# F on its own hardware queue, k quads in column tiles, and w2 and w3 of the first chunk by contraction halves in a Linformer attention and maxout kernel

## The chip, the cores and the metric

One core of one Trainium2 chip. The metric is the device time of one execution in microseconds (us), the median of several. The span that a profile shows is some 1.8 us shorter than that time.

## The reference, cut to what matters

```python
# batch 8, heads 8, sequence 1024, head_dim 64, k_proj 64
k_proj = np.einsum('ks,bhsd->bhkd', E, k)        # E, F: (64, 1024)
v_proj = np.einsum('ks,bhsd->bhkd', F, v)
attn   = softmax(q @ k_proj.T / 8)
x      = attn @ v_proj                           # -> (8192, 512)
h      = max(max(x @ w1, x @ w2), x @ w3)        # w1..w3: (512, 768)
out    = h @ w_out                               # (768, 512)
```

## The kernel before: the parts that matter

Batches are taken one after the other, each in two chunks of 512 tokens. While batch b runs through the maxout layer, the attention of batch b+1 is slipped in between its steps. Only the start is special: nothing can be overlapped with batch 0, so its first chunk has its own code, and all three edits are in it.

The loads of batch 0, in the order of issue. All but E and F go through POOL's software queue:

```python
    nc.sync.dma_start(out=ef_f[0:KP], in_=E)
    nc.sync.dma_start(out=ef_f[KP:P], in_=F)
    # ... on POOL: q and k (4 heads at a time), v of heads 0-1, 2-3, 4-5
    load_w(0, slice(0, 2))            # w1, first half of the contraction
    load_kv(2, V3)                    # v of heads 6-7
    load_w(0, slice(2, 3)); load_w(0, slice(3, 4))
    load_w(1, slice(0, 2)); load_w(1, slice(2, 4))      # w2
    load_w(2, slice(0, 2))                              # w3, first half
    load_q(ALL, slice(SPC, SI))                         # q of the second chunk
    load_w(2, slice(2, 4))                              # w3, second half
    # ... w_out, then batch 1            (written one call to a line in the kernel)
```

The k projection of four heads, its transpose, and the start of the front. `idle(n)` is n filler matmuls on a tile of zeros, there to keep PE's clock up:

```python
    def k_duo(u):
        t, ns = bank()
        for si in range(SI):
            nc.tensor.matmul(out=t[0:KP, 0:4 * D], lhsT=efT[:, si, 0:KP],
                             rhs=k_t[:, 4 * u:4 * u + 4, si, :], ...)
        kp0[u] = att.tile([KP, 4 * D], BF16, name="kp0")
        copy("v", kp0[u], t[0:KP, 0:4 * D], ns, 0.45)
    # kt_duo: two transposes of kp0, one copy
    k_duo(0); q_duo(1); kt_duo(0); idle(1)
    # scores of two head pairs, their sums; then the second four heads, v, ...
```

The first chunk of the maxout layer (`NJT` = 6 column tiles jt, `NCT` = 4 contraction tiles ct). The first weight goes ct by ct; the other two go jt by jt, and VectorE takes the running maximum from the PSUM bank as each jt ends. Keys such as `(2, 5)` name the step behind which attention work of the second chunk is put:

```python
        for i in (1, 2):                                  # w2, w3
            for jt in jts:
                t, ns = bank()
                up_mm(t, i, 0, 0, jt, range(NCT))
                most(hs[:, jt] if i == 1 else hTs[0, 0][:, jt, :], t, ns, hs[:, jt])
                then((i, jt))
        # work: (2, 0), (2, 1): transposes of q (qp); (2, 2), (2, 3): scores (sc);
        # (2, 5): sums, values, and the multiply into xT on VectorE (za), scores
```

The softmax here doesn't subtract the row's maximum and nothing guards it: scores larger than these inputs give would overflow.

## Time and profile before

| | |
|---|---|
| time, median of 3 | 409.4 us (409.08 to 409.49) |
| span, PE busy | 407.8 us, 394.0 us (97%) |
| granted TensorE clock | 0.997 |

The page of the kernel before. Its last line here is a group of equal instructions: behind the first bar its busy time in us and the mean of one in ns, behind the second how long the engine stood idle just before them, and what ended most of that:

```profile
span 407.8 us, 5967 instructions
PE 394.0 (97%) x2381; PEld 180.1 (44%) x2425; DVE 201.5 (49%) x309; ACT 191.2 (47%) x278; POOL 31.4 (8%) x44
...
L502 PE MATMUL banks<-xT,w_sb 128*128 128x512 bf16 x1118 | 254.6, 379 | 2.6 <-DMA w_sb<-in_moe_w_dram 0.6
```

PE is the bound, so a gain can come only from time in which PE stands or does filler. The chain of waits of the kernel before, first 50 us (start, length, what):

```profile
6.35 0.66 POOL v_t L143
7.01 13.44 DMA w_sb<-in_moe_w_dram
20.45 0.28 issue
20.73 13.09 DMA w_sb<-in_moe_w_dram
33.82 0.04 issue
33.87 0.61 PE banks L502 x2
...
48.39 0.99 PE banks L280 x16
```

From 7.01 to 33.87 us it is the load stream, and from then on mostly PE. The timeline of the kernel before (start, length, engine, line, operation, tiles, shapes, and in brackets the idle time before it):

```profile
10.91 1.03 PE L402 MATMUL banks<-k_t,efT 128*64 128x256 bf16 x8 [0.62 <-DMA k_t<-in_k_dram]
11.98 0.42 DVE L99 CAST kp<-banks 64x256 bf16<-64x256 f32 x1 [1.94 <-PE banks L402]
12.23 0.64 PE L291 MATMUL banks<-ident,q_t 128*64 128x128 bf16 x16 [0.28 <-DMA q_t<-in_q_dram]
12.80 0.23 PE L415 MATMUL banks<-ident,kp 64*128 64x64 bf16 x2
12.91 0.69 DVE L99 COPY qT<-banks 128x1024 bf16<-128x1024 bf16 x1 [0.51 <-PE banks L291]
13.51 0.21 DVE L99 COPY kpT<-banks 128x128 bf16<-128x128 bf16 x1
13.78 0.41 PE L199 MATMUL banks<-qT,kpT 64*64 64x256 bf16 x8 [0.76 <-DVE kpT L99]
...
21.51 2.10 PE L502 MATMUL banks<-xT,w_sb 128*128 128x512 bf16 x9
...
33.87 0.61 PE L502 MATMUL banks<-xT,w_sb 128*128 128x512 bf16 x2 [0.62 <-DMA w_sb<-in_moe_w_dram]
```

The k projection (10.91) waits for k; the transpose of its result (12.80) waits behind transposes of q, which wait for q, and the copy of that (13.51) behind the copy of q's transposes on VectorE (12.91); the first up matmul (21.51) comes 1.06 us after w1's first half landed (20.45); and in the middle of w3 PE stands for its second half.

Throughout this text a load "lands" when the last of the sixteen counts of its semaphore arrives, as the trace records them.

### The profile page before, as it was taken

The numbers are of one execution on the slowest core, as the hardware profiler recorded it, in microseconds if no ns is written. First come the engines' busy times: TensorE is split into PE (matmuls) and PEld (weight loads), VectorE is DVE, ScalarE is ACT, GpSimd is POOL, SyncE is SP. The second block draws the span as 40 slices with busy tenths as digits, with TensorE's granted clock in tenths as the row PEclk, the third lists the DMA queues.
The fourth block names the chain that finished last, engine by engine and source line by source line (L and its number), as shares of the span: only waits on it lengthen the run. The fifth ranks groups of instructions, "written<-read, shape, count | busy, mean of one in ns | idle before, by whom it ended". The sixth has DMA issues, their size and how long they took to land.

```text
span 407.8 us, 5967 instructions
## 1 busy us (share of the span) xinstructions
PE 394.0 (97%) x2381; PEld 180.1 (44%) x2425; DVE 201.5 (49%) x309; ACT 191.2 (47%) x278; POOL 31.4 (8%) x44
## 2 busy tenths in 40 slices
PE   7899999999999999999999999999999999999995
PEld 2543453344444544444544445444544444444443
DVE  2357665473565527636453555525464363525251
ACT  2531538624764266556544555437535555432322
POOL 7421002002000200200200002000000000000000
PEclk9999999999999999999999999999999999999998
DMA  8999939949916994892798119950510202020202
GB/s 150 205 205 207 232 88 154 250 113 139 245 30 190 172 251 110 130 241 45 207 181 179 54 24 244 204 147 2 139 70 1 104 0 104 0 104 0 103 2 104
DMA packets 58508, 52.30 MB, mean 128 GB/s; under 512 B 25968, under 2 KB 54128, under 8 KB 58480
## 3 DMA queue, kind: packets, MB, share of 16 engines
q0 software_dynamic: 28512, 28.31, 43.6%
q1 hardware_dynamic: 29824, 23.46, 17.6%
q8 instruction: 19, 0.31, 0.3%
q10 hardware_dynamic: 144, 0.13, 0.1%
q14 instruction: 9, 0.07, 0.1%
HBM read 57.15 MB, written 16.78 MB: 181 GB/s over the span
## 4 chain that ended last, share of the span: by engine, by line
PE 87%; DMA 7%; ACT 2%; POOL 1%; issue 1%; DVE 1%; DVEq 0%; ACTq 0%; POOLq 0%
PE banks L502 58%; PE banks L593 19%; DMA w_sb<-in_moe_w_dram 7%; PE banks L219 4%; PE banks L280 3%; PE banks L199 2%; PE banks L291 1%; POOL v_t L143 1%; DMA out_dram<-o_sb 0%; ACT zi L238 0%; ACT zl L232 0%; POOL k_t L143 0%; ACT pT L210 0%; POOL q_t L148 0%; DVE hT L512 0%
## 5 line engine op out<-in xcount | busy, mean ns | idle before, releaser
L502 PE MATMUL banks<-xT,w_sb 128*128 128x512 bf16 x1118 | 254.6, 379 | 2.6 <-DMA w_sb<-in_moe_w_dram 0.6
L502 PEld LDWEIGHTS <-w_sb 128*128 128x128 bf16 x1152 | 109.7, 98 | 137.6 <-issue 10.1
L558 DVE TENSOR_TENSOR m<-banks,h1s 128x512 f32<-128x512 f32 x90 | 62.0, 689 | 86.0 <-ACT h1s L554 54.6
L554 ACT COPY h1s<-banks 128x512 f32<-128x512 f32 x90 | 52.5, 583 | 92.5 <-PE banks L502 89.2
L593 PE MATMUL banks<-wout_sb,hT 128*128 128x512 bf16 x370 | 85.0, 379 | 0.9 <-issue 0.3
L249 DVE TENSOR_TENSOR xT<-banks,zi 128x1024 bf16<-128x1024 f32 (+1 forms) x36 | 39.8, 1106 | 77.2 <-ACT zi L238 57.9
L512 DVE TENSOR_TENSOR hT<-banks,m 128x512 bf16<-128x512 f32 x90 | 62.3, 692 | 10.1 <-DVE m L558 0.5
L99 ACT COPY o_sb<-banks 128x512 f32<-128x512 f32 (+1 forms) x60 | 34.9, 581 | 53.3 <-PE banks L593 53.2
L593 PEld LDWEIGHTS <-hT 128*128 128x128 bf16 x378 | 35.9, 98 | 45.9 <-DVE hT L512 3.3
L232 ACT ACTIVATE zl<-banks 128x1024 f32<-128x1024 f32 (+1 forms) x36 | 33.5, 930 | 30.9 <-PE banks L219 30.7
L210 ACT ACTIVATE pT<-banks 128x1024 bf16<-128x1024 f32 (+1 forms) x36 | 33.2, 931 | 15.3 <-PE banks L199 15.3
L238 ACT ACTIVATE zi<-zl 128x1024 f32<-128x1024 f32 (+1 forms) x36 | 34.6, 962 | 1.1
L188 POOL DMA_DIRECT2D q_t<-in_q_dram x7 | 6.1, 878 | 205.1 <-DMA qT<-q_p 108.1
L219 PE MATMUL banks<-pT,ones 64*64 64x512 bf16 (+1 forms) x144 | 13.9, 376 | 0.9 <-DVE xT L249 0.3
L199 PE MATMUL banks<-qT,kpT 64*64 64x512 bf16 (+1 forms) x144 | 13.0, 359 | 1.1 <-DVE kpT L99 0.8
L219 PE MATMUL banks<-pT,vp 64*64 64x512 bf16 (+1 forms) x144 | 13.3, 355 | 0.2
L280 PEld LDWEIGHTS <-efT 128*64 128x64 bf16 x224 | 11.7, 110 | 2.7 <-issue 2.7
L219 PEld LDWEIGHTS <-ones 64*64 64x64 bf16 x144 | 4.4, 103 | 15.1 <-issue 14.7
L99 DVE CAST vp<-banks 64x256 bf16<-64x256 f32 (+1 forms) x18 | 7.1, 395 | 5.8 <-ACT vp L99 3.4
L373 PE MATMUL banks<-warm 128*128 128x512 bf16 x23 | 8.5, 502 | 1.2 <-DVE warm L166 1.2
L99 ACT CAST vp<-banks 64x256 bf16<-64x256 f32 x14 | 5.1, 365 | 7.3 <-PE banks L280 7.1
L99 DVE COPY q_p<-q_t 128x1024 bf16<-128x1024 bf16 x24 | 8.5, 419 | 0.0
(48 smaller groups left out, 107.0 us busy)
## 6 DMA issues: line engine op xcount, KB each, us to landing
out_dram<-o_sb SPq DMA_DIRECT2D x30, 512.0 KB, 3.5
k_t<-in_k_dram POOLq DMA_DIRECT2D x7, 1024.0 KB, 14.4
q_t<-in_q_dram POOLq DMA_DIRECT2D x7, 1024.0 KB, 9.7
v_t<-in_v_dram POOLq DMA_DIRECT2D x7, 1024.0 KB, 18.7
w_sb<-in_moe_w_dram POOLq DMA_DIRECT2D x5, 384.0 KB, 11.7
k_t<-in_k_dram POOLq DMA_DIRECT2D x2, 512.0 KB, 9.9
v_t<-in_v_dram POOLq DMA_DIRECT2D x4, 256.0 KB, 12.3
wout_sb<-in_moe_w_out_dram POOLq DMA_DIRECT2D x1, 768.0 KB, 15.6
```

The costliest lines, as they stand in the source:

```text
L99: done = {"v": nc.vector.tensor_copy, "s": nc.scalar.copy, "g": nc.gpsimd.tensor_copy}[eng](out=o, in_=i)
L210: nc.scalar.activation(out=pTs[b, g, lo], in_=t, func=AF.Exp, scale=scale)
L219: nc.tensor.matmul(out=t[hp * HALF:(hp + 1) * HALF, c, 0:nsi * HALF], lhsT=w(rows, hp), rhs=p[rows, hp, :], start=True, stop=True,)
L232: nc.scalar.activation(out=zl, in_=t, func=AF.Ln)
L238: nc.scalar.activation(out=zi, in_=zl, func=AF.Exp, scale=-1.0)
L249: nc.vector.tensor_tensor(out=xTs[b][:, g, lo:lo + nsi, :].rearrange("a (c s) p -> a c (s p)", c=2), in0=t, in1=zi, op=ALU.mult,)
L280: nc.tensor.matmul(out=t[hh * HALF:(hh + 1) * HALF, 0:width], lhsT=efT[:, si, (kv - 1) * KP:kv * KP], rhs=qkv[b][kv][:, heads[hh], si, :], ...
L502: nc.tensor.matmul(out=h, lhsT=w_sb[i][:, ct, jt * P:(jt + 1) * P], rhs=xTs[b][:, ct, ch * SPC:(ch + 1) * SPC, :], start=(ct == first), st ...
L512: nc.vector.tensor_tensor(out=o, in0=h, in1=other, op=ALU.max)
L554: nc.scalar.copy(out=h1s, in_=h[0][0])
L558: nc.vector.tensor_tensor(out=m12, in0=h[1][0], in1=h1s, op=ALU.max)
L593: nc.tensor.matmul(out=o_ps, lhsT=hTs[b, ch][:, jt, tt * P:(tt + 1) * P], rhs=wout_sb[:, jt, :], start=(jt == 0), stop=(jt == NJT - 1),)
```

## The change

"k quads" is the name for the k projection of four heads in two column tiles: two of the heads are written to rows 0 to 63 of the result and two to rows 64 to 127, where all four went to rows 0 to 63 before. "The halves" are w2 and w3 of the first chunk, done by halves of the contraction.

Intent: have E and F in sooner, shorten the way to the first scores and hence to the first up matmul, and give PE work that does not need w3's second half until it has landed.

```diff
-    nc.sync.dma_start(out=ef_f[KP:P], in_=F)
+    nc.scalar.dma_start(out=ef_f[KP:P], in_=F)
 # k_duo: two column tiles, each two heads of the four
-        for si in range(SI): nc.tensor.matmul(out=t[0:KP, 0:4 * D], ...)
-        kp0[u] = att.tile([KP, 4 * D], BF16, name="kp0")
+        proj(0, 1, t, (slice(4 * u, 4 * u + 2), slice(4 * u + 2, 4 * u + 4)), 2 * D)
+        kp0[u] = att.tile([P, 2 * D], BF16, name="kp0")
 # kt_duo: one 128x128 transpose instead of two
 # the front
     k_duo(0)
-    at(10.3)
-    q_duo(1)
+    idle(2)
     kt_duo(0)
     idle(1)
     # ... scores of two head pairs
-    idle(2)
+    at(10.6)
+    q_duo(1)
 # w2 and w3 of the first chunk
         for i in (1, 2):
+            h = []
             for jt in jts:
-                t, ns = bank()
-                up_mm(t, i, 0, 0, jt, range(NCT))
-                most(..., t, ns, hs[:, jt])
+                h.append(bank())
+                up_mm(h[jt][0], i, 0, 0, jt, range(NCT // 2))
+                then((i, "a", jt))
+            for jt in jts:
+                up_mm(h[jt][0], i, 0, 0, jt, range(NCT // 2, NCT))
+                most(..., *h[jt], hs[:, jt])
                 then((i, jt))
 # attention work behind them: (2, 0), (2, 1) -> (2, "a", 2), (2, "a", 5);
 # (2, 2), (2, 3), (2, 5) -> (2, 0), (2, 2), (2, 4)
```

More of the change, by code (lines that the diff above doesn't have):

```diff
@@ L400, in k_duo @@
         t, ns = bank()
-        for si in range(SI):
-            nc.tensor.matmul(
-                out=t[0:KP, 0:4 * D], lhsT=efT[:, si, 0:KP],
-                rhs=k_t[:, 4 * u:4 * u + 4, si, :],
-                start=(si == 0), stop=(si == SI - 1),
-            )
-        pe(0.9)
-        kp0[u] = att.tile([KP, 4 * D], BF16, name="kp0")
-        copy("v", kp0[u], t[0:KP, 0:4 * D], ns, 0.45)
+        proj(0, 1, t, (slice(4 * u, 4 * u + 2), slice(4 * u + 2, 4 * u + 4)), 2 * D)
+        kp0[u] = att.tile([P, 2 * D], BF16, name="kp0")
+        copy("v", kp0[u], t[:, 0:2 * D], ns, 0.3)
     def kt_duo(u):
@@ L413, in kt_duo @@
         t = t.bitcast(BF16)
-        for gg in range(2):
-            nc.tensor.transpose(
-                out=t[:, gg * KP:(gg + 1) * KP],
-                in_=kp0[u][:, gg * P:(gg + 1) * P], identity=ident[0:KP, 0:KP],
-            )
+        nc.tensor.transpose(out=t[:, 0:P], in_=kp0[u], identity=ident)
         pe(0.15)
@@ L421, in kt_duo @@
             "v", kpTs[0][:, 2 * u:2 * u + 2, :].rearrange("a g k -> a (g k)"),
-            t[:, 0:2 * KP], ns, 0.25,
+            t[:, 0:P], ns, 0.25,
         )
@@ L475 @@
     z(1)
+    idle(1)
     at(12.8)
@@ L479 @@
     kt_duo(1)
-    at(14.3)
+    at(14.1)
     v_pair(0)
@@ L533, in up_first @@
         for i in (1, 2):
+            h = []
             for jt in jts:
-                t, ns = bank()
-                up_mm(t, i, 0, 0, jt, range(NCT))
-                most(hs[:, jt] if i == 1 else hTs[0, 0][:, jt, :], t, ns, hs[:, jt])
+                h.append(bank())
[3 more added lines that the diff above has]
+                up_mm(h[jt][0], i, 0, 0, jt, range(NCT // 2, NCT))
+                most(hs[:, jt] if i == 1 else hTs[0, 0][:, jt, :], *h[jt], hs[:, jt])
                 then((i, jt))
@@ L683 @@
                     (0, 1, 5): [lambda: x(3)],
-                    (2, 0): [qp(0, (0, 1), *c1)],
-                    (2, 1): [qp(0, (2, 3), *c1)],
-                    (2, 2): [sc(0, 0, *c1)],
-                    (2, 3): [sc(0, 1, *c1)],
-                    (2, 5): [za(0, 0, *c1), sc(0, 2, *c1)],
+                    (2, "a", 2): [qp(0, (0, 1), *c1)],
+                    (2, "a", 5): [qp(0, (2, 3), *c1)],
+                    (2, 0): [sc(0, 0, *c1)],
+                    (2, 2): [sc(0, 1, *c1)],
+                    (2, 4): [za(0, 0, *c1), sc(0, 2, *c1)],
                 })
```

## The prediction

> **What bounds the kernel now.** TensorE: the page gives PE 394.0 of 407.8 us busy, clock 0.997. Of the 13.8 us idle, 6.1 lie in the first 60 us (busy time by stretches). All three edits act in the first 42 us. There the load stream bounds: the software queue moves some 205 GB/s without a pause from 7 to 48 us, and the chain of waits is a w_sb load from 7.0 to 20.5 and another from 20.7 to 33.8. In the timeline PE follows landings: k projection at 10.91 (k landed 10.87), first up matmul 21.51 (w1 half landed 20.45), and a stall to 33.87 for the second half of w3 (landed 33.83).
>
> **The change, costed.**
>
> 1. F on its own queue. F was issued at 1.38, its packets flowed from 3.6 to 5.2, after E's, and it landed at 7.07; in 4.0 to 5.2 the software queue got only about 60 KB where it later moves 200 KB/us. The Trainium skill ("DMA: Bandwidth & Descriptors", Queues, rings and completion order) says SP and ACT each own a row of rings on the same 16 engines. So E and F should flow together from 2.2 and F land near 5. The engine work is not less; it fills a half-empty start. Estimate: every later load lands 0.6 us earlier (0.2 to 0.8), w3's second half near 33.2. The E/F transposes then wait for the identity (POOL, 6.35): 6.4 instead of 7.83, but the k projection still waits for k, about 10.3.
>
> 2. k quads. Eight 128x256 matmuls in 1.03 us become 16 of 128 columns, in pairs of column tiles, about 0.55 us (32 of 256 columns take 1.87 elsewhere); the copy 0.42 -> 0.29; one transpose for two. And q_duo(1), which waited for q until 12.23 and held the k transpose back to 12.80, moves behind the scores. First scores 13.78 -> 11.9, second 17.86 -> about 15.9. But first up then waits for w1 (20.45 - 0.6): 21.51 -> 19.9. These two steps together bring PE 1.6 us forward; the loads set it.
>
> 3. ct halves. 12 matmuls (2.6 us) of w3 stand before its second half is needed, so the stall to 33.87 (PE group 0.62 idle, PEld 1.1) goes. No arithmetic changes. But results come in bunches: w2's six maxima (0.69 each, 0.61 to 0.79 apart) fall due within 2.6 us of PE, so VectorE runs about 2 us behind. The second q transpose must wait for a pair of banks (six are open), and the last hT maximum stands behind a 0.69 us xT multiply that waits for ScalarE. PE arrives at the first down step about 2 us early and there waits, I estimate, 0.7 us before its sixth matmul; another 0.3 to 0.4 us is lost at the scores.
>
> **On the path.** About 2 us won by 40 us, half given back to VectorE: 1.0 us kept. After that all is paced by PE and moves along (k, q, v of batch 1 land 4 to 5 us before use).
>
> **Time: 408.4 us**, 407.6 to 409.1 (8 in 10). Faster by over 2%: 0.01; within 2%: 0.98; slower: 0.01.
>
> **Right or wrong.** F landing 4.5 to 5.3; w3's second half at 33.0 to 33.5 and no PE wait for it; first up matmul 19.6 to 20.2; in the first down step a wait for DVE hT, 0.4 to 1 us; the first k projection of batch 1 (48.39) at 47.2 to 47.7; every later stage the same length.
>
> **What would make it wrong.** The load stream not shifting (gain 0.4 or less); VectorE keeping up better, so the whole 2 us stays (407.4); bank waits worse than I count (no gain). If ACT's issue delays its table load or casts, it is hidden.

## The result, and the profile after

| | before | after |
|---|---|---|
| time, median of 4 | 409.28 us | 408.63 us (408.55 to 409.40) |
| ratio, 95% interval | | 0.9988 (0.9971 to 1.0006) |

A ratio here is the mean time of one kernel's fast runs over that of the other's fast runs of the same rounds, so it is not quite the ratio of the medians. The interval includes 1: by these runs alone the kernels are the same. The change was run twice more below; over the three times, 15 executions of it have a mean of 408.90 us and the 24 of the kernel before beside them 409.15 us, each with a scatter (standard deviation) of 0.42 us. So the question is not why the gain is large or small, but what lies under a quarter of a microsecond of net gain: parts that cancel, or parts that do nothing.

The page of the changed kernel, profiled in the slowest of those four executions:

```profile
span 407.6 us, 5997 instructions
PE 393.7 (97%) x2395; PEld 180.1 (44%) x2440; DVE 201.1 (49%) x309; ACT 191.2 (47%) x278; POOL 31.5 (8%) x44
...
L588 PE MATMUL banks<-wout_sb,hT 128*128 128x512 bf16 x370 | 85.1, 379 | 1.6 <-DVE hT L503 0.9
```

The down matmuls now stand 1.6 us in all, 0.9 of it for hT on VectorE; in the kernel before it was 0.9 us, the largest part of which, 0.3, was for nothing the profile shows. (L493 and L588 here are L502 and L593 of before, L503 is L512.) Its timeline:

```profile
10.49 0.64 PE L280 MATMUL banks<-k_t,efT 128*64 128x128 bf16 x16 [1.11 <-DMA k_t<-in_k_dram]
11.16 0.29 DVE L99 CAST kp<-banks 128x128 bf16<-128x128 f32 x1 [2.04 <-PE banks L280]
11.51 0.23 PE L408 MATMUL banks<-ident,kp 128*128 128x128 bf16 x1
11.78 0.23 DVE L99 COPY kpT<-banks 128x128 bf16<-128x128 bf16 x1 [0.33 <-PE banks L408]
12.06 0.41 PE L199 MATMUL banks<-qT,kpT 64*64 64x256 bf16 x8
12.40 0.64 PE L291 MATMUL banks<-ident,q_t 128*64 128x128 bf16 x16
...
20.79 2.12 PE L493 MATMUL banks<-xT,w_sb 128*128 128x512 bf16 x9
...
30.06 3.68 DVE L503 TENSOR_TENSOR hs<-banks,hs 128x512 f32<-128x512 f32 x6 [2.07 <-PE banks L493]
...
36.73 0.30 PE L199 MATMUL banks<-qT,kpT 64*64 64x256 bf16 x4 [0.25 <-DVE qT L99]
...
40.23 1.24 PE L588 MATMUL banks<-wout_sb,hT 128*128 128x512 bf16 x5
40.83 0.69 DVE L249 TENSOR_TENSOR xT<-banks,zi 128x512 bf16<-128x512 f32 x1 [0.73 <-ACT zi L238]
41.44 0.68 DVE L503 TENSOR_TENSOR hT<-banks,hs 128x512 bf16<-128x512 f32 x1
42.18 0.39 PE L588 MATMUL banks<-wout_sb,hT 128*128 128x512 bf16 x1 [0.70 <-DVE hT L503]
```

The first scores come 1.7 us sooner than before (12.06 against 13.78). VectorE stands 2.07 us for lack of a finished bank and then takes six maxima in a row. Five matmuls of the first down step run at 40.23, and the sixth stands 0.70 us for the last hT maximum, which stood behind a multiply that waited for ScalarE.

### The whole run in four pieces

The traces of all runs let the run be cut at three points: the first up matmul of the first chunk, the first k projection of batch 1 (at 48.3 us in the kernel before), and the last matmul. The last long piece, from that k projection to the last matmul, is 354.99 to 355.02 us in **every one** of the fourteen profiles. So all that the change does must be in the first two pieces:

| us | first up matmul at | from there to the k projection of batch 1 | from there to the last matmul | end |
|---|---|---|---|---|
| before | 21.51 | 26.81 | 354.99 | 4.5 |
| after, three profiles | 20.79, 20.32, 20.03 | 27.30, 27.29, 27.29 | 355.0 | 4.5 to 4.6 |

The first piece became shorter by 0.7 to 1.5 us and scatters; the second became **longer** by 0.48 us and scatters by 0.01. The experiments take these apart.

### The profile page after: what moved, and what is told of

It reads as the page before. It is cut to its first block, busy times and chain, and to the rows that moved or that the text cites. A ratio compares the mean times of both kernels' runs of the same rounds, so it can differ in the third digit from the quotient of the medians.

```text
span 407.6 us, 5997 instructions
## 1 busy us (share of the span) xinstructions
PE 393.7 (97%) x2395; PEld 180.1 (44%) x2440; DVE 201.1 (49%) x309; ACT 191.2 (47%) x278; POOL 31.5 (8%) x44
## 4 chain that ended last, share of the span: by engine, by line
PE 89%; DMA 4%; ACT 2%; DVE 2%; issue 2%; POOL 1%; DVEq 0%; ACTq 0%; POOLq 0%
PE banks L493 60%; PE banks L588 19%; PE banks L219 4%; PE banks L280 3%; DMA v_t<-in_v_dram 3%; PE banks L199 2%; DVE hT L503 1%; PE banks L291 1%; ACT zl L232 1%; DMA out_dram<-o_sb 0%; ACT zi L238 0%; POOL k_t L143 0%; ACT pT L210 0%; POOL q_t L148 0%; POOL v_t L143 0%
## 5 line engine op out<-in xcount | busy, mean ns | idle before, releaser
L493 PE MATMUL banks<-xT,w_sb 128*128 128x512 bf16 x1118 | 254.5, 379 | 2.1 <-issue 0.6
L493 PEld LDWEIGHTS <-w_sb 128*128 128x128 bf16 x1152 | 109.5, 98 | 136.8 <-issue 10.1
L588 PE MATMUL banks<-wout_sb,hT 128*128 128x512 bf16 x370 | 85.1, 379 | 1.6 <-DVE hT L503 0.9
L503 DVE TENSOR_TENSOR hT<-banks,m 128x512 bf16<-128x512 f32 x90 | 62.3, 692 | 10.1 <-DVE m L553 0.5
L588 PEld LDWEIGHTS <-hT 128*128 128x128 bf16 x378 | 36.0, 98 | 46.9 <-DVE hT L503 4.4
L210 ACT ACTIVATE pT<-banks 128x1024 bf16<-128x1024 f32 (+1 forms) x36 | 33.2, 931 | 14.7 <-PE banks L199 14.7
L280 PEld LDWEIGHTS <-efT 128*64 128x64 bf16 x256 | 12.8, 110 | 4.5 <-issue 4.0
L280 PE MATMUL banks<-k_t,efT 128*64 128x256 bf16 (+1 forms) x144 | 8.7, 263 | 1.2 <-DMA k_t<-in_k_dram 1.1
```

Source lines behind the costliest of these rows:

```text
L210: nc.scalar.activation(out=pTs[b, g, lo], in_=t, func=AF.Exp, scale=scale)
L280: nc.tensor.matmul(out=t[hh * HALF:(hh + 1) * HALF, 0:width], lhsT=efT[:, si, (kv - 1) * KP:kv * KP], rhs=qkv[b][kv][:, heads[hh], si, :], ...
L493: nc.tensor.matmul(out=h, lhsT=w_sb[i][:, ct, jt * P:(jt + 1) * P], rhs=xTs[b][:, ct, ch * SPC:(ch + 1) * SPC, :], start=(ct == first), st ...
L503: nc.vector.tensor_tensor(out=o, in0=h, in1=other, op=ALU.max)
L588: nc.tensor.matmul(out=o_ps, lhsT=hTs[b, ch][:, jt, tt * P:(tt + 1) * P], rhs=wout_sb[:, jt, :], start=(jt == 0), stop=(jt == NJT - 1),)
```

## The experiments

Each was timed in five rounds beside the kernel before: the first four of the table, the next four, the next three, and the last, each on one chip. Kernels are compared only within the same rounds. "Load" below is always the landing of w1's first half, which the first up matmul needs.

| run | time, median | ratio to before (95%) | load lands | first up at | second piece |
|---|---|---|---|---|---|
| again | 409.24 | 0.9999 (0.9984 to 1.0014) | 20.27 | 20.32 | 27.29 |
| no_f | 409.02 | 1.0002 (0.9985 to 1.0019) | 19.93 | 20.54 | 27.28 |
| no_kquad | 409.61 | 1.0021 (0.9998 to 1.0043) | 20.72 | 20.83 | 27.29 |
| no_halves | 409.59 | 1.0010 (0.9995 to 1.0025) | 20.67 | 20.75 | 27.79 |
| max_first | 408.93 | 0.9986 (0.9974 to 0.9999) | 20.25 | 20.29 | 26.79 |
| q_last | 408.63 | 0.9978 (0.9965 to 0.9992) | 19.75 | 19.79 | 26.64 |
| q_last_no_f | 408.22 | 0.9977 (0.9964 to 0.9990) | 20.39 | 20.43 | 26.59 |
| only_halves | 409.71 | 1.0005 (0.9991 to 1.0018) | 18.84 | 21.45 | 27.28 |
| trio | 408.02 | 0.9973 (0.9960 to 0.9987) | 20.18 | 20.22 | 26.41 |
| trio_no_f | 407.94 | 0.9972 (0.9960 to 0.9985) | 19.64 | 19.69 | 26.72 |
| again2 | 408.68 | 0.9989 (0.9977 to 1.0002) | 19.98 | 20.03 | 27.29 |
| no_kquad2 | 409.49 | 1.0010 (0.9986 to 1.0034) | 20.45 | 21.03 | 27.28 |

All were correct. Most of these times differ by less than their scatter; it is the pieces of the trace that decide.

### again, again2: the changed kernel unedited

> The changed kernel once more, for a second profile and a better time. The first profile was taken in its slowest execution of four (409.40 us against 408.55 to 408.69). Theory (VectorE gives back): 408.5 to 408.8 us, 0.5 to 0.9 us under the kernel before; in the profile PE waits 0.5 to 0.9 us for the last hT maximum before the sixth matmul of the first down step. Rival (the load stream alone sets the gain): no such wait in this execution, and the first k projection of batch 1 moves by exactly as much as the last w1 landing.

> The changed kernel a third time, beside these two on one chip. Theory: 27.28 to 27.30 us for the stretch, 0.70 us of PE wait for the last hT maximum, first up matmul within 0.1 us of the landing of w1's first half; 0.2 to 0.8 us faster than before, the difference to before set by how late that load lands.

The times scattered as said, 408.43 to 409.61 us and 408.43 to 409.01. The median of `again` missed what was written (409.24, level with before); that of `again2` was 0.44 us under before. The second piece was 27.29 us both times, and the wait for the last maximum 0.70 us both times. The chain of waits of again2:

```profile
7.08 12.90 DMA w_sb<-in_moe_w_dram
19.98 0.05 issue
20.03 2.12 PE banks L493 x9
...
35.22 0.70 DVE qT L99
...
39.40 0.64 ACT zi L238
40.06 0.04 DVE xT L249
40.10 0.57 issue
40.67 0.69 DVE hT L503
41.37 0.05 issue
41.41 0.39 PE banks L588
```

One load instead of two; then PE; and where the kernel before has PE from 33.87 to 41.1, VectorE and ScalarE stand in the chain. In all three profiles the first up matmul starts 0.05 us after its load. The rival, that the load stream alone sets the gain, is half right: it sets the first piece; VectorE and ScalarE stand in the chain of the second.

### no_halves: the change without the ct halves

```diff
-            (halves: two loops over jt, six banks open)
+            (the old loop: one bank, four ct, one maximum)
```

> The changed kernel with w2 and w3 of the first chunk done jt by jt again, one bank at a time. Theory: PE waits 1.0 to 2.0 us for the second half of w3 (33.4 to 34.3), but VectorE then keeps up and the wait of 0.7 us before the sixth matmul of the down step is gone; 0.1 to 0.6 us slower than the changed kernel. Rival (the halves carry the gain): 0.7 us or more slower.

The second piece became 27.79 us, 0.50 longer than with the halves. The waits of PE between 20 and 50 us show why (who waited, for whom, us in all, times, longest):

```profile
PE banks L493 <- DMA w_sb<-in_moe_w_dram: 1.4, 2, 1.0
```

PE stands 0.4 us for w2's second half and 1.0 us for w3's, and not at all for hT. As the theory said; 0.35 us slower in the median than `again`, within the scatter.

### only_halves: the kernel before with the halves alone

> The kernel before with the halves alone. Theory: first up matmul 10.60 us after the first k projection as in the kernel before, PE-bound (about 21.5), then 27.29 us as in the changed kernel: the k projection of batch 1 at 48.6 to 49.0 us, 0.3 to 0.7 us later than in the kernel before, whose wait for w3 it trades for the waits on VectorE. Rival (removing the wait for w3 is a gain by itself): 47.6 to 48.1.

```profile
PE banks L597 <- DVE hT L512: 0.7, 1, 0.7
```

The second piece is 27.28 us again, although everything before it is the old code and the first up matmul came 0.7 to 1.4 us later than in the changed kernel (at 21.45 as in the kernel before, though by another way: k landed at 9.14, but the clock was at one half from 7.57 to 10.99 us, and the first k projection ran at 11.29; so it was 10.16 us ahead of the first up matmul, not the 10.60 expected): the k projection of batch 1 came at 48.73 us, against 48.32 before. So the halves are worth **-0.50 us behind the new front and +0.47 us behind the old one**. Behind the old front PE reached w3 later, waited less for it (0.62 us idle), and the halves cost more on VectorE than that. Behind the new front PE would wait 1.4 us, and the halves cost less than that.

### max_first: the last maximum ahead of the multiply

```diff
-                    (2, 4): [za(0, 0, *c1), sc(0, 2, *c1)],
+                    (2, 5): [za(0, 0, *c1), sc(0, 2, *c1)],
```

> The changed kernel with the attention step of the second half-batch one place later, so that the last hT maximum stands ahead of the xT multiply on VectorE. Theory (a give-back on VectorE behind that multiply): the 0.70 us wait before the sixth down matmul goes, and the stretch from the first up matmul to the first k projection of batch 1, 27.29 us in both profiles of the changed kernel, becomes 26.5 to 26.8. Rival (PE must wait elsewhere anyway, for instance for ScalarE's Ln and Exp in the down steps): 27.2 to 27.4. The time follows within what the load stream scatters (0.8 us between executions).

The second piece became 26.79 us: 0.50 shorter, at the far end of what was written. The wait for the last hT maximum was indeed gone, but a part of it came back as another:

```profile
40.12 1.46 PE L588 MATMUL banks<-wout_sb,hT 128*128 128x512 bf16 x6 [0.53 <-ACT zl L232]
```

The down step's bank is one that ScalarE still has to read. So both the theory and the rival hold a part: 0.86 us of spacing lost at the sixth matmul, 0.50 regained. This one-line edit alone brings the second piece back to what it is in the kernel before (26.81), whose order of matmuls still had to wait for w3.

### no_kquad, no_kquad2: the change without the k quads

> The changed kernel with the old k projection and the old order of k, q and scores. Theory: PE comes to the first up matmul 0.7 to 1.0 us later than in the changed kernel, behind the landing of w1, and as the halves crowd VectorE's maxima, the delay is kept: 1.0 to 1.6 us slower than the changed kernel, so 0.4 to 0.9 us slower than before. Rival (the front is hidden behind the loads): as fast as the changed kernel within 0.2 us.

> The changed kernel with the old k projection and order once more, as its first run said less than expected: first up matmul 10.60 us after the first k projection, and only 0.11 us behind the load of w1's first half. Theory: old order PE-bound at 10.60 us after the first k projection in every execution, whereas in the changed kernel that distance is 9.55 to 10.31 us and set by the load; so the k quads are worth what the load leaves of 10.60, 0.1 to 1.0 us, and this run shows 10.55 to 10.65 us, then 27.29 us. Rival (the load hides the front in both): the first up matmul within 0.05 us of the load, at a distance other than 10.60.

Both take back the new order of k, q and scores along with the quads. The first expectation, 1.0 to 1.6 us slower than the changed kernel, was too high: 0.37 us in the median beside `again`, within the scatter. The second run's timeline:

```profile
10.41 1.03 PE L402 MATMUL banks<-k_t,efT 128*64 128x256 bf16 x8 [1.30 <-DMA k_t<-in_k_dram]
...
21.03 2.10 PE L502 MATMUL banks<-xT,w_sb 128*128 128x512 bf16 x9
```

With the old k part the first up matmul comes 10.60 (before), 10.61 and 10.62 us after the first k projection, though it is 1.06, 0.11 and 0.58 us behind its load; in only_halves, at half clock for a part of it, it was 10.16. With the quads it comes 10.30, 10.03 and 9.55 us after it in the changed kernel, and each time 0.05 us behind its load. So the old front was not bound by the load, and the new one is. What the quads and the new order are worth is what the load leaves of those 10.6 us, an estimated 0.3 to 1.05 us in these three profiles. Their own floor was not reached in any of them.

No run parts the quads from the new order, but the two timelines shown above do it for the first scores. From the first k projection to them it was 2.87 us before and 1.57 after. Of the 1.30 us, 0.53 are the quads' (0.40 up to the copy of the result, 0.13 in that copy) and 0.78 the order's: the transpose followed the copy by 0.40 us and now by 0.06, and its own copy, held up by q's, followed it by 0.71 us and now by 0.27. So at this place the moved transposes of q gave more than the quads.

### no_f, q_last_no_f, trio_no_f: F behind E again

```diff
-    nc.scalar.dma_start(out=ef_f[KP:P], in_=F)
+    nc.sync.dma_start(out=ef_f[KP:P], in_=F)
```

> The changed kernel with F issued behind E on the old queue again. Theory: F's own queue moves the landings of k, q and v by some 0.4 us and no more, and that reaches the end one to one only as far as the first up matmul waits for w1: 0.0 to 0.4 us slower than the changed kernel. Rival (the gain is F's): 0.6 us or more slower, back at the time of before.

Here `no_f` is the change with that line put back; the other two are told below. The times could not tell them apart: against before 1.0002 beside 0.9999 for `again`, and in the median 0.22 us under `again`, where 0.0 to 0.4 slower was written and 0.6 or more by the rival. The landings do say something. Nine profiles have F on its own queue and five have it behind E (before, only_halves and these three):

| us | F lands | first software packet | k lands, mean | load lands, mean (range) |
|---|---|---|---|---|
| F on its own queue, 9 | 5.66 to 5.95 | 3.63 to 4.13 | 10.29 | 20.33 (19.75 to 20.74) |
| F behind E, 5 | 5.55 to 7.07 | 2.93 to 3.35, once 4.09 | 9.94 | 19.85 (18.84 to 20.45) |

The own queue makes F's landing early and steady. It does not make the other loads earlier; on average they were 0.4 us later, with ranges that overlap (0.2 for the load without only_halves, whose early landing is told below). With it the software queue's first packet mostly comes 0.7 us later, as if E and F together held it back instead of filling a gap. By 7 us (`--dma --window 0:7`) the software queue had moved 0.43 MB in the kernel before, and 0.43, 0.40 and 0.45 MB in the three profiles of the change: nothing was gained at the start. That fits the Trainium skill ("DMA: Bandwidth & Descriptors", Issuing engines are not separate DMA queues): DMAs of several issuers run on the same 16 engines, and issuing from several saves only issue time. That section should have weighed more in the prediction than the one on rings. Whether F's own queue really delays the load is not settled by fourteen profiles of different kernels. In q_last_no_f and trio_no_f F landed at 5.59 and 5.55 us although it was behind E, so these two did not test PE's wait for F.

A load lands with the slowest engine. The same page (Why a DMA increments its semaphore by 16 and not by 1) says that the participating engines finish independently; here the sixteen counts of one load spread over 1.1 to 2.3 us from k's landing on in the four profiles that I took apart so (before, after, again, no_f), and an engine that falls behind seems mostly to stay behind (the counts do not name their engine). In the changed kernel's first profile the last count of v (heads 4-5) was 1.01 us behind the one before it, where for the load ahead of it it was 0.16 behind; and an instruction fetch of 16 KB that took 0.95 us had started on the DMA engines at 17.08 us, between the two. That the fetch sat on that engine is an inference from the times, but it holds up: in every one of the fourteen profiles such a fetch starts between 15.67 and 18.84 us, and the load then under way, or the next, has one lagging count more than the load before. In only_halves the first fetch starts at 18.70; all sixteen counts of w1's first half had lain within 0.29 us, which gave the earliest landing of all, 18.84, and those of the next load lie 1.41 us apart. It would explain why one kernel's load lands at 19.98 or 20.74.

There is one more effect. In `no_f` PE stood 1.72 us for F and its casts, and the granted clock fell to one half:

```profile
core 0: us, PE busy (x) PEld busy (x) DVE busy (x) ACT busy (x) POOL busy (x), PEclk, DMA share, GB/s
5.40:8.80 3.40, 1.68 (x27) 1.10 (x26) 0.85 (x2) 0.66 (x2) 2.97 (x6) 1.00 1.28 200
8.90:12.20 3.30, 3.30 (x22) 1.41 (x21) 1.00 (x3) 0.44 (x1) 1.10 (x2) 0.50 1.31 205
12.30:15.70 3.40, 3.27 (x54) 1.80 (x52) 0.97 (x3) 2.23 (x4) 1.15 (x2) 1.00 1.24 205
```

From 8.85 to 12.27 us PE ran at half clock, 3.41 us, which agrees with the window of 3413 ns that the Trainium skill gives ("TensorE: Matmul & The Clock Gate", Part 1). Five filler matmuls took 2.26 us there, and 1.25 in the changed kernel; the first up matmul came 0.60 us after its load, where it comes 0.04 to 0.08 after it in the other kernels with the quads. Two of the five profiles with F behind E show this, none of the nine with F on its own queue. But one execution in six of each no_kquad run, with F on its own queue, took 412.27 and 412.22 us, at a clock of 0.992 and 0.989, so the own queue doesn't rule a lower clock out.

### q_last: the old jt order, with q after w3

```diff
     load_w(2, slice(0, 2))
-    load_q(ALL, slice(SPC, SI))
     load_w(2, slice(2, 4))
+    load_q(ALL, slice(SPC, SI))
 # w2, w3 jt by jt as before; q transposes and scores behind (2, 1) to (2, 4), not (2, 0) to (2, 3)
```

> F on its own queue and k quads kept; w2 and w3 jt by jt again, but the q load of the second half-batch issued after the second half of w3, and its transposes one step later. Theory: the old order of matmuls is the shorter one (26.07 us from the first up matmul to the k projection once the 0.75 us wait of before is taken off) and was only held up by the landing of w3, which now comes 2.65 us earlier; so 26.0 to 26.4 us for that stretch and no wait for w3 nor for the last hT maximum, about 1 us shorter than the changed kernel. Rival (the halves are needed to keep PE busy whatever the order of loads): 27 us or more.

> The same with F behind E on the old queue. Theory (F's own queue holds the software queue back at the start: its first packet at 3.75 to 4.02 us in four profiles, 3.15 to 3.19 in the two without it): first software packet at 3.1 to 3.3, and w1's first half lands 0.2 to 0.7 us earlier than in the runs with F on its own queue (20.27 to 20.74). But F then lands at 6.8 to 7.1 and PE stands from 6.1 to 7.5, which lets its clock fall back in some executions. Rival (F's own queue speeds the loads): w1's first half lands later than 20.7.

If the halves are there only because w3 lands late, then landing w3 sooner must do without them. The second piece was 26.64 and 26.59 us, 0.65 to 0.70 shorter than with the halves. The expectation was 26.0 to 26.4; what was left is in PE's waits of q_last:

```profile
PE banks L493 <- DMA w_sb<-in_moe_w_dram: 0.7, 2, 0.4
```

Nothing for w3 or hT, but 0.4 us for w2's second half (and 0.3 us at the first up matmul). The expected landing in q_last_no_f, 0.2 to 0.7 us ahead of all those with F on its own queue, did not come: 20.39.

### trio: w2 by halves, three banks at a time

```diff
+        for trio in (jts[:3], jts[3:]):
+            h = {}
+            for jt in trio:
+                h[jt] = bank()
+                up_mm(h[jt][0], 1, 0, 0, jt, range(NCT // 2))
+            for jt in trio:
+                up_mm(h[jt][0], 1, 0, 0, jt, range(NCT // 2, NCT))
+                most(hs[:, jt], *h[jt], hs[:, jt])
 # then w3 jt by jt, q late, as in q_last
```

> The kernel with the late q load (F on its own queue, k quads, w3 jt by jt), and w2 by halves over three banks at a time instead of jt by jt. In that kernel the one PE wait left was 0.40 to 0.45 us for the second half of w2 (landed 26.77). Theory: it goes and nothing comes back on VectorE, as only three maxima fall due together: first up matmul to first k projection of batch 1 26.1 to 26.4 us, against 26.64, and 27.29 in the changed kernel. Rival (any halves cost VectorE's lag): 26.6 or more. Time 0.9 to 1.5 us under the kernel before.

> The same with F behind E. Theory: the same stretch of 26.1 to 26.4; first software packet at 2.9 to 3.4 us against 3.6 to 4.0; w1's first half lands no later than with F on its own queue, so the time is the same within 0.5 us, unless PE's clock falls back while it waits for F. Rival (F's own queue speeds the loads): 0.5 us or more slower than with it.

The second piece was 26.41 us with F on its own queue, at the very edge of what was written, and 26.72 with F behind E, outside it. The first software packet of trio_no_f came at 4.09 us, also not as written. The wait for w2 is gone and no wait for VectorE came, but the late q is now the next in line:

```profile
PE banks L291 <- DMA q_t<-in_q_dram: 0.3, 1, 0.3
```

In trio_no_f that wait is 0.63 us: the first up matmul started 0.54 us earlier there and q landed only 0.22 us earlier (33.33 against 33.55). Both are clear of 1: 0.9973 (0.9960 to 0.9987) and 0.9972 (0.9960 to 0.9985), beside 0.9989 for the change on the same chip. trio is the fastest version with the change's F and quads, 408.02 us against 408.68 for the change and 409.12 for before. All five of its times lie under all five of `again2`. Its own F variant is no different.

## Why the prediction was right or wrong

- **The time**, 408.4 us with a range of 407.6 to 409.1: 408.63 us lies in it, and same within 2% was right. The gain of 1.0 us was too large: 0.65 us by the medians, 0.25 us between the means of all 15 and 24 executions.
- **Step 1, the term that was mis-sized**: "every later load lands 0.6 us earlier (0.2 to 0.8), w3's second half near 33.2". Against the one profile of before, k landed 0.42, 0.61 and 0.42 us earlier in the three profiles of the change, w1's first half 0.29 later, 0.18 and 0.47 earlier, w3's second half 0.51 later, 0.03 and 0.47 earlier, a mean of 0.0. "F land near 5" was 5.67 to 5.94. In its place: the software queue's first packet came at 3.94 to 4.13 us instead of 3.19, and by 7 us that queue had moved as much as before (0.40 to 0.45 MB for 0.43); F's own first packet came at 3.1 us, not with E's at 2.1 to 2.3. I had counted the bytes that F took from the software queue later, but not that the software queue would start later. Over all profiles with this order of loads w3's second half shows no gain either: the seven with F on its own queue have it at 34.01 us in the mean, the three with F behind E at 33.43.
- **Step 2, the k quads**: right in kind and in its durations (0.64 us for 0.55; the copy 0.29; first scores 12.06 for 11.9). Right too that the first up matmul then waits for its load: 0.05 us behind it in three of three. Its time, 19.6 to 20.2, held in one of three, by the load.
- **Step 3, the halves**: right, and the closest: no PE wait for w3, and in its place a wait for the last hT maximum of 0.70 us (estimate 0.7), and 0.25 us at the scores with some 0.16 more beside it (estimate 0.3 to 0.4). VectorE's six maxima took 3.68 us for PE's 2.6. What I did not see was the sum: over the old order the halves are a loss of 0.47 us unless PE reaches w3 early (only_halves, no_halves).
- **"All moves along after that"**: right to 0.03 us in 355. The k projection of batch 1, written for 47.2 to 47.7, came at 48.09, 47.61 and 47.32.

So the first piece won about 1.1 us (21.51 to 20.38, the mean of three), the second lost 0.48. About 2 us and 1 us were predicted: both came to about half, and that the time still lay in its range owes something to this. The sum, 0.65 us, happens to be the difference of the medians; with one profile of before and a load stream that scatters by as much, its size is less sure than its two signs.

## What to carry to other kernels

When a stall is covered by reordering, compare the whole stretch, not the stall: the halves removed a wait of 0.62 us on a load and brought 0.95 us of waits on VectorE, as results that used to come one at a time came six together. Ask first whether the awaited load can stand earlier in its queue; here that, and w2 by halves over three banks instead of six, brought 0.66 us more than the change (408.02 against 408.68), which itself had 0.44 over before. And with a scatter of 0.4 us, cut the traces at fixed points: the pieces that do not depend on the load stream repeated to 0.03 us, and showed what the timed rounds here did not.

## What the Trainium skill lacked or had wrong

- "DMA: Bandwidth & Descriptors": that the software queue can start later beside loads on both hardware queues is not there. First software packet 3.63 to 4.13 us with E and F on two hardware queues (9 profiles), 2.93 to 3.35 with both on one (4 of 5; the fifth 4.09).
- The same page tells that the engines of one DMA finish independently, but gives no size: 1.1 to 2.3 us between first and last count of loads of 256 to 512 KB in the four profiles taken apart, and 0.3 us in only_halves until 18.84; a lag once got is mostly kept by the later loads (2.02 to 2.11 us from 20.74 to 32.23 in the first profile of the change).
- No page says by how much an instruction fetch can hold up a load: a packet of 16 KB took 0.88 to 1.05 us (first 50 us of before and after), near a lag of one engine of about the same size.
- "TensorE: Matmul & The Clock Gate" says that the clock falls after an idle window of about 3.4 us; here it fell at 8.85 us (no_f) after a window from 5.44 in which PE stood only 1.72 us at a stretch and was busy, mostly with transposes, for 1.7 of 3.4 us, while in the kernel before it stood 1.76 us at a stretch and the clock held. The page's remark that transposes may not count as PE-busy fits, and was not tested.
